# A state-space convolution and a mixer MLP on one core: weights by signed length and angle, constants on Pool, one ScalarE table ahead of the first turn

## The chip, the cores and the metric

The kernel runs on one core of one Trainium2 chip. The metric is device time in microseconds of one execution, lower is better; shown is the median of several runs. The kernel before takes 714.86 us (three runs, 712.22 to 715.42).

## The reference

Two blocks work on a sequence of 2048 positions with 512 channels, each scaled and shifted by values that come from a condition vector. The first block is a long convolution whose kernel K is the sum of 128 damped oscillations per channel. Cut to what matters:

```
mod = (silu(c) @ w_mod).reshape(1, 6, 1, 512)           # w_mod is 512 x 3072
sa, ca, ga, sb, cb, gb = mod[:, 0], ..., mod[:, 5]
h = layernorm(x) * (1 + ca) + sa
# first block: A, B, C are complex, 512 x 128
dt = exp(log_dt)
P  = exp((dt * A)[:, :, None] * l[None, None, :])       # l = 0 .. 2047
K  = einsum("dn,dnl,dn->dl", C, P, dt * B).real         # 512 x 2048
y  = irfft(rfft(h, padded) * rfft(K, padded)) + h * Dskip
x  = x + ga * y
h  = layernorm(x) * (1 + cb) + sb
x  = x + gb * mixer(h)      # spatial shift, then a channel MLP 512 -> 1376 -> 512
```

For the change it matters that the weight of one oscillation, w = C * B * dt, is complex. The kernel writes it as a length times a turn by an angle: the length multiplies the exponential's magnitude, the angle is added to the phase of the oscillation, and the oscillation is then one sine.

## The kernel before, in words

All the code is in `body`, in stages. The diff lies in the first.

Preparation (lines 285 to 409, a schedule written by hand: the order of the calls is the order on each engine). SP loads log_dt, c and the six raw arrays of A, B and C; Pool waits for one of them (`gate`) and then loads constant matrices (PA, CE, C0, PB, C1) on its own queue. VectorE builds two constants, MG and ON, in `cst`, then dt (`exp_exact`), then `la` (log magnitude per step) and `tf`, `t64` (phase per step and per 64 steps, each reduced by `frac` to a fraction of a turn), then the weight w as `wr`, `wi`. `hi` (a copy on ScalarE that rounds) and `lo` (a subtraction on VectorE) split each into two parts in `hilo`. `place` and `parts` are matmuls with 0/1 matrices that move these parts to the layout of later matmuls: TES (magnitudes), T0S (phase per step) and T1S (phase per 64 steps and the weight's angle). `exps` makes exponentials of magnitudes, four of 1024 columns and one of 768.

The angle of w is found from min/max of |wr| and |wi|: an arctangent of their quotient (`at0`), and then corrections by octant and quadrant with three masks `sg`, `sw`, `si`. The length is max * cos + min * sin of that arctangent, `wn`.

Modulation: `load_mod(n)` loads a 512-column block of w_mod (1 MB), `mod_parts(n)` multiplies it with the condition in four column groups and copies the result, `mod_sum(n)` adds the four groups. Blocks 0 to 2 are needed by the first block.

Rounds (`for k in range(33)`): `turns(k, cos)` makes the phase of one group of oscillations in PSUM, with rounding to whole turns by adding and subtracting the constant MAGIC = 1.5 * 2^23 through matmuls with ON and MG, and ScalarE takes the sine; `products(k)` on VectorE multiplies with the exponentials; `burst(k)` sums over oscillations by matmuls into K, held in the tile KX. Two `turns` run ahead of `products`. Each step of a turn is a pair of matmuls: l0 (phase per step, 32 rows of each group, zero-padded in the constant C0 to 64) into one half of a PSUM tile, l1 (64 rows of the other half of the array) into the other half. Between the rounds `side[k]` places the normalisation of u, its transforms, and more loads. After the rounds come the transforms of K and u, the products, the inverse transform and the mixer.

`psx` has two buffers: `turns`, `exps` and `parts` share them.

Of the kernel before, what the change touches and what calls it, by code (L numbers as in the profile page):

```python
# [14 lines left out]
MAGIC = 12582912.0  # L15
# [12 lines left out]
def shape_constants():  # L28
# [35 lines left out]
    c0 = np.tile((eye[:, :, None] * (j + .5)).reshape(16, 512), (2, 1))  # L64
    C0 = np.zeros((2, 2, 32, 2, 512))
    C0[:, 0, :, 0], C0[:, 1, :, 1] = c0, c0
    C0 = C0.reshape(128, 1024)
# [44 lines left out]
def body(ctx, tc, A):  # L112
# [6 lines left out]
    def act(out, in_, f=AF.Copy, scale=1.0, bias=0.0):  # L119
        return S.activation(out, in_, f, bias=bias, scale=scale)  # L120
# [73 lines left out]
    C0 = ph.tile([128, 1024], F32R, name="C0")  # L194
    C1 = ph.tile([128, 512], F32R, name="C1")
    CE = ph.tile([128, NXC], F32R, name="CE")
    C0N = ph.tile([128, 1024], F32R, name="C0N")
    C1N = ph.tile([128, 512], F32R, name="C1N")
    MG = ph.tile([128, 512], F32R, name="MG")
    ON = ph.tile([128, 3, 128], F32R, name="ON")  # L200
# [80 lines left out]
    def frac(x, r):  # L281
        V.tensor_scalar(r, x, MAGIC, MAGIC, op0=OP.add, op1=OP.subtract)
        V.tensor_sub(x, x, r)

    with tc.manual_schedule():
# [12 lines left out]
        V.memset(DS, 0.0)  # L298
# [4 lines left out]
        for r in (32, 96):  # L303
            V.memset(cst[r:r + 32], 1.0)
        V.tensor_copy(MG, cst)
        V.memset(cst[:, :384], 0.0)
        for i, (r, v) in enumerate(((0, 1.0), (0, -1.0), (32, 0.25))):
            for q in (r, r + 64):
                V.memset(cst[q:q + 1, i * 128:i * 128 + 128], v)
        V.tensor_copy(ON.rearrange("p a b -> p (a b)"), cst[:, :384])  # L310
        V.tensor_scalar(ld[:, 4:], cT, -1.0, None, op0=OP.mult)
        ex = exp_exact(pp, ld, [128, 8], "dt")
        dt = ex[:, :4]
# [24 lines left out]
        lo(0, tf)  # L338
# [3 lines left out]
        place(TES, 6, PA)  # L342
# [4 lines left out]
        V.tensor_mul(wr, cr, br)  # L347
        V.tensor_mul(t0, ci, bi)
        lo(2, t64)
        V.tensor_sub(wr, wr, t0)  # L350
        V.tensor_mul(wi, cr, bi)
        V.tensor_mul(t1, ci, br)
        V.tensor_add(wi, wi, t1)
        exps(0, 0, 5)
# [4 lines left out]
        def parts(i0, i1):  # L359
            for v in range(4):  # L360
                for i in range(i0, i1):
# [4 lines left out]
        ax, ay, mn = cr, br, tmp("mn")  # L366
        V.scalar_tensor_tensor(ax, wr, -1.0, wr, op0=OP.mult, op1=OP.max)
        V.scalar_tensor_tensor(ay, wi, -1.0, wi, op0=OP.mult, op1=OP.max)
        mx, mc = tmp("mx"), tmp("mc")
        V.tensor_tensor(mc, ax, ay, op=OP.max)  # L370
        V.tensor_scalar(mx, mc, 1e-37, None, op0=OP.max)
        V.reciprocal(mx, mx)
        V.tensor_tensor(mn, ax, ay, op=OP.min)
        V.tensor_mul(mx, mn, mx)
        at, at0 = tmp("at"), tmp("at0")
        act(at0, mx, AF.Arctan)
        act(at, at0, scale=INV2PI)
        act(wn, at0, AF.Sin, scale=-1.0, bias=hpi)
        act(ws, at0, AF.Sin)
        mp = [mod_parts(n) for n in range(2)]  # L380
        for f in mp:
            f()
        for n in range(2):
            mod_sum(n)()
        load_mod(2)
        load_u(0)
        sg, sw, si = la, t0, t1
        V.tensor_tensor(sg, ay, ax, op=OP.is_gt)
        V.tensor_scalar(sg, sg, -2.0, None, op0=OP.mult)
        V.tensor_scalar(sw, wr, 0.0, -2.0, op0=OP.is_lt, op1=OP.mult)  # L390
        V.tensor_scalar(si, wi, 0.0, -2.0, op0=OP.is_lt, op1=OP.mult)
        V.scalar_tensor_tensor(at, sg, 1.0, at, op0=OP.add, op1=OP.mult)
        V.scalar_tensor_tensor(at, sg, -0.125, at, op0=OP.mult, op1=OP.add)
        V.scalar_tensor_tensor(at, sw, 1.0, at, op0=OP.add, op1=OP.mult)
        V.scalar_tensor_tensor(at, sw, -0.25, at, op0=OP.mult, op1=OP.add)
        V.scalar_tensor_tensor(at, si, 1.0, at, op0=OP.add, op1=OP.mult)
        V.scalar_tensor_tensor(at, tf, 31.5, at, op0=OP.mult, op1=OP.add)
        frac(at, rr)
        hi(4, at)
        lo(4, at)  # L400
        parts(2, 4)
        for i in range(2):
            act(T1S.rearrange("p (t v) n -> p v t n", v=4)[:, 2 * i:2 * i + 2],
                px[i].rearrange("p (v t n) -> p v t n", v=2, t=4))
        V.tensor_mul(wn, wn, mc)
        V.tensor_mul(ws, ws, mn)
        V.tensor_add(wn, wn, ws)
        V.tensor_tensor(as4(wn), as4(wn), by(dt), op=OP.mult)
    pr.close()
# [38 lines left out]

    def turns(k, cos):
        t, u = divmod(k, 4)  # L450
        r0 = slice(u // 2 * 64, u // 2 * 64 + 64)
        r1 = slice(64 - r0.start, 128 - r0.start)
        l0, l1, c = T0S[r0, t], T1S[r1, t * 2 + k % 2], slice(k % 2 * 512, k % 2 * 512 + 512)
        x = psx.tile([128, 1024], F32, name="xx")
        ops = [(l0, C0[r0, c], l1, C1[r1])] + [(ON[r0, i], MG[r0], ON[r1, i], MG[r1]) for i in (2, 0, 1)[1 - cos:]]
        ops.append((l0, C0N[r0, c], l1, C1N[r1]))
        for i, (la, ma, lb, mb) in enumerate(ops):
            T.matmul(x[:, :512], la, ma, start=(i == 0), stop=(i == len(ops) - 1))  # L458
            T.matmul(x[:, 512:], lb, mb, start=(i == 0), stop=(i == len(ops) - 1))  # L459
# [80 lines left out]
    with tc.manual_schedule():  # L540
# [3 lines left out]
        for i in range(4):  # L544
            T.transpose(wps[:, i * 128:i * 128 + 128], wn[:, i * 128:i * 128 + 128], ident)
        act(WN, wps)
        late = mod_parts(2)
        turns(1, 0)
        late()
        late = mod_sum(2)  # L550
        turns(1, 1)
        late()
        load_u(1)
        for k in range(33):
            now, later = later, []
# [30 lines left out]
            for f in side[k]:  # L586
                f()
# [682 lines left out]
```

## Time and profile before

| | |
|---|---|
| median of 3 runs | 714.86 us (712.22 to 715.42) |
| profiled execution: its time | 714.44 us |
| its span, first to last instruction | 712.6 us |
| TensorE clock granted, mean | 0.994 |
| busy in the span | TensorE 669.5 us, VectorE 506.6, ScalarE 335.5, Pool 86.7 |
| 0 to 13 us | TensorE 0, VectorE 10.40, ScalarE 2.54 us busy |
| 13 to 38 us | TensorE 18.10, VectorE 22.44, ScalarE 17.64 us busy |

PE is TensorE's matmuls, PEld its weight loads, DVE is VectorE, ACT is ScalarE, SP issues DMAs. A row of the timeline begins with its start and its busy time in us, then engine, line, operation, out<-in and shapes; what stands in brackets is the idle time before it and what ended it. A matmul's end is modelled, so it is its start that counts. A mark like 64*128 behind a matmul is the rows and columns of the array that it uses. Line numbers are those of the kernel before; L120 is the helper for all of ScalarE's activations.

### The profile page before, as it was taken

The numbers are of one execution on the slowest core, as the hardware profiler recorded it, in microseconds if no ns is written. First come the engines' busy times: TensorE is split into PE (matmuls) and PEld (weight loads), VectorE is DVE, ScalarE is ACT, GpSimd is POOL, SyncE is SP. The second block draws the span as 40 slices with busy tenths as digits, with TensorE's granted clock in tenths as the row PEclk, the third lists the DMA queues.
The fourth block names the chain that finished last, engine by engine and source line by source line (L and its number), as shares of the span: only waits on it lengthen the run. The fifth ranks groups of instructions, "written<-read, shape, count | busy, mean of one in ns | idle before, by whom it ended". The sixth has DMA issues, their size and how long they took to land.

```text
span 712.6 us, 16838 instructions
## 1 busy us (share of the span) xinstructions
PE 669.5 (94%) x7083; PEld 516.9 (73%) x7083; DVE 506.6 (71%) x847; ACT 335.5 (47%) x549; POOL 86.7 (12%) x191
## 2 busy tenths in 40 slices
PE   2689999999999999998999899999999999999997
PEld 1256555656569665664688889999898988989896
DVE  8889999999996666866988868557464636454422
ACT  3769888889866444533344623314123221212120
POOL 1011211112000000000473100101010000000000
PEclk9899999999999999999999999999999999999999
DMA  8451374653439999874659201011020101111011
GB/s 280 145 144 52 91 218 101 181 139 94 141 75 332 237 301 302 267 241 152 204 176 319 90 22 39 16 45 31 27 63 16 53 22 31 31 30 30 0 30 30
DMA packets 56627, 85.51 MB, mean 120 GB/s; under 512 B 5508, under 2 KB 43400, under 8 KB 54888
## 3 DMA queue, kind: packets, MB, share of 16 engines
q1 hardware_dynamic: 52536, 66.87, 33.2%
q0 software_dynamic: 3136, 16.52, 6.5%
q8 instruction: 56, 0.92, 0.6%
q10 hardware_dynamic: 880, 1.05, 0.5%
q14 instruction: 19, 0.16, 0.1%
HBM read 58.20 MB, written 31.85 MB: 126 GB/s over the span
## 4 chain that ended last, share of the span: by engine, by line
PE 47%; DMA 2%; DVE 2%; ACT 1%; issue 1%; SPq 1%; ACTq 0%; DVEq 0%
PE pm L824 7%; PE pm L825 7%; PE pm L827 7%; PE pa L948 6%; PE pa L940 6%; PE pa L941 6%; PE ph L878 2%; PE ph L879 2%; PE ph L881 2%; PE pT L789 2%; DMA ld<-ZT 1%; DMA GD<-go 1%; PE pT L1138 1%; PE py L721 1%; DMA win<-GD 0%
## 5 line engine op out<-in xcount | busy, mean ns | idle before, releaser
L120 ACT ACTIVATE gh<-pm 128x512 fp32r<-128x512 f32 (+1 forms) x48 | 26.9, 561 | 200.6 <-PE pm L827 200.6
L824 PE MATMUL pm<-nh,w3h 128*128 128x256 f32 (+1 forms) x352 | 85.8, 279 | 0.9 <-ACT nh L120 0.9
L825 PE MATMUL pm<-nh,w3l 128*128 128x256 f32 (+1 forms) x352 | 85.6, 279 | 0.1
L932 DVE TENSOR_TENSOR gl<-gf,gh 128x512 fp32r<-128x512 f32 (+1 forms) x48 | 30.9, 643 | 68.3 <-ACT gf L120 68.3
L940 PE MATMUL pa<-w4h,gh 128*128 128x512 f32 (+1 forms) x176 | 69.6, 395 | 0.0
L941 PE MATMUL pa<-w4l,gh 128*128 128x512 f32 (+1 forms) x176 | 68.9, 392 | 0.0
L824 PEld LDWEIGHTS pm<-nh,w3h 128*128 128x128 f32 (+1 forms) x352 | 65.3, 185 | 2.6 <-ACT nh L120 1.1
L825 PEld LDWEIGHTS pm<-nh,w3l 128*128 128x128 f32 (+1 forms) x352 | 65.2, 185 | 2.2 <-DVE w3l L743 0.5
L827 PE MATMUL pm<-nl,w3h 128*128 128x256 f32 (+1 forms) x352 | 54.8, 277 | 0.0
L948 PE MATMUL pa<-w4h,gl 128*128 128x512 f32 (+1 forms) x176 | 48.1, 390 | 0.8 <-DVE gl L932 0.8
L458 PE MATMUL xx<-MG,ON 64*128 64x512 f32 x160 | 47.0, 389 | 0.0
L459 PE MATMUL xx<-MG,ON 64*128 64x512 f32 x160 | 47.0, 389 | 0.0
L827 PEld LDWEIGHTS pm<-nl,w3h 128*128 128x128 f32 (+1 forms) x352 | 46.6, 185 | 0.2 <-DVE nl L797 0.2
L752 POOL TENSOR_TENSOR rs<-mv,eps_t 128x1 f32<-128x1 f32 (+1 forms) x39 | 11.9, 306 | 278.0 <-DVE mv L758 266.1
L884 DVE TENSOR_TENSOR h<-h,ph 128x512 f32<-128x512 f32 x16 | 11.0, 688 | 45.1 <-PE ph L881 45.1
L476 DVE SCALAR_TENSOR_TENSOR e<-tr,p 128x512 f32<-128x512 f32 x64 | 41.1, 683 | 1.8 <-ACT tr L120 1.8
L120 ACT ACTIVATE z<-pz 128x512 f32<-128x512 f32 x32 | 17.4, 594 | 51.4 <-issue 21.7
L677 DVE TENSOR_TENSOR ma<-pk,us 128x512 f32<-128x512 f32 x32 | 21.9, 686 | 26.8 <-issue 15.8
L508 PEld LDWEIGHTS kp<-e,e 128*32 128x32 f32 x2048 | 30.1, 110 | 12.9 <-issue 7.2
L948 PEld LDWEIGHTS pa<-w4h,gl 128*128 128x128 f32 (+1 forms) x176 | 33.0, 188 | 8.3 <-DVE gl L932 1.2
L485 DVE TENSOR_TENSOR e<-tr,p 128x1024 f32<-128x1024 f32 x32 | 39.0, 1218 | 0.0
L486 DVE TENSOR_TENSOR e<-tr,m 128x1024 f32<-128x1024 f32 x32 | 39.0, 1218 | 0.0
(234 smaller groups left out, 1755.6 us busy)
## 6 DMA issues: line engine op xcount, KB each, us to landing
VU<-vs SPq DMA_DIRECT2D x64, 128.0 KB, 3.2
ld<-VU SPq DMA_DIRECT2D x16, 512.0 KB, 14.1
ZT<-z POOLq DMA_DIRECT2D x15, 512.0 KB, 7.1
ld<-ZT SPq DMA_DIRECT2D x12, 512.0 KB, 5.5
Dw<-in_w POOLq DMA_DIRECT2D x8, 688.0 KB, 4.7
xu<-in_u SPq DMA_DIRECT2D x16, 256.0 KB, 5.7
KX<-in_u SPq DMA_DIRECT2D x16, 256.0 KB, 12.3
GD<-go SPq DMA_DIRECT2D x16, 256.0 KB, 2.5
```

Of the source, the lines that this page charges most:

```text
L120: return S.activation(out, in_, f, bias=bias, scale=scale)
L458: T.matmul(x[:, :512], la, ma, start=(i == 0), stop=(i == len(ops) - 1))
L459: T.matmul(x[:, 512:], lb, mb, start=(i == 0), stop=(i == len(ops) - 1))
L476: V.scalar_tensor_tensor(e0[:, 1, a], tr[:, 1, 0], 1.0 - 2.0 * a, mg[:, a], op0=OP.mult, op1=OP.mult)
L485: V.tensor_mul(e0[:, 0], tr[:, 0, 0:1].to_broadcast([128, 2, 512]), mg)
L486: V.tensor_mul(e1.rearrange("p r d q -> p r (d q)"), tr[:, :, 1], m1s[0][:, u % 2:u % 2 + 1].to_broadcast([128, 2, 512]))
L824: T.matmul(p, wh[:, k, c], hi[k], start=(k == 0), stop=False)
L825: T.matmul(p, wl[:, k, c], hi[k], start=False, stop=False)
L827: T.matmul(p, wh[:, k, c], lo[k], start=False, stop=(k == 3))
L940: T.matmul(acc[i], gh[:m, e, s], W4h[:m, f], start=(f == 0), stop=False)
L941: T.matmul(acc[i], gh[:m, e, s], W4l[:m, f], start=False, stop=False)
L948: T.matmul(acc[i], gl[:m, e, s], W4h[:m, f], start=False, stop=(f == 10))
```

## The change

Five things are done at once.

- The angle is taken to the nearer axis: the larger of wr and wi becomes the signed divisor, so the quotient is signed and its arctangent lies within an eighth of a turn; a quarter turn is added where wi is larger (`sg`). The half turn for a negative divisor is left out, as the length keeps its sign. Two predicated copies take the place of the chain of corrections; |wr|, -wr and |wi| are made on ScalarE.
- MG and ON are built on Pool. MG is the same in all rows, and ON exists in two forms, for 32 rows and for 64.
- C0 has 512 columns in place of 1024. `turns` takes the 32 rows of l0 alone, beside the 64 rows of l1 in the other half.
- Modulation blocks 0 to 2 are loaded into KX, K's tile, behind the load of Dskip; both first tiles of u are loaded right behind them. `mod_sum` 0 and 1 and all of block 2 move behind the first turns.
- One element of sine ahead of the arctangent makes one table serve both.

```diff
-    C0 = np.zeros((2, 2, 32, 2, 512))
-    C0[:, 0, :, 0], C0[:, 1, :, 1] = c0, c0
+    c0 = np.tile((eye[:, :, None] * (j + .5)).reshape(16, 512), (4, 1))
+    C0 = np.tile(c0, (2, 1))
...
     def load_mod(n):
-        wmt[n] = (up if n < 3 else wml).tile([128, 4, 512], F32, name="xu" if n < 3 else "wm")
+        wmt[n] = KX[:, n * 2048:n * 2048 + 2048].rearrange("p (a b) -> p a b", a=4) if n < 3 else \
+            wml.tile([128, 4, 512], F32, name="wm")
...
-        load_mod(0)
-        load_mod(1)
-        V.memset(DS, 0.0)
-        for j in range(4):
-            Y.dma_start(DS[32 * j:32 * j + 1], A["dk"][j:j + 1])
+        P.memset(cst, MAGIC / 3)
+        P.tensor_copy(MG, cst)
+        for j in range(2):
+            P.memset(cst[:, :384], 0.0)
+            for i, v in enumerate((3.0, -3.0, 0.75 / MAGIC)):
+                for q in range(0, 128, 32 + 32 * j):
+                    P.memset(cst[q:q + 1, i * 128:i * 128 + 128], v)
+            P.tensor_copy(ON[:, j].rearrange("p b c -> p (b c)"), cst[:, :384])
-        V.memset(cst, MAGIC)
...
         frac(tf, rr)
+        V.memset(DS, 0.0)
+        for j in range(4):
+            Y.dma_start(DS[32 * j:32 * j + 1], A["dk"][j:j + 1])
+        load_mod(0)
+        load_mod(1)
+        load_mod(2)
+        load_u(0)
+        load_u(1)
...
-        place(T0S, 0, PA)
+        lo(0, tf)
+        act(ax, wr, AF.Abs)
+        act(nr, wr, scale=-1.0)
+        act(ay, wi, AF.Abs)
         exps(0, 0, 5)
+        place(T0S, 0, PA)
+        act(t31, tf, scale=31.5)
         act(C0N, C0.bitcast(F32), scale=-1.0)
         act(C1N, C1.bitcast(F32), scale=-1.0)
+        act(ws[:, :1], hpi, AF.Sin)
...
-        parts(0, 2)
...
+        parts(range(4), 0)
+        mp = [mod_parts(0)]
+        V.tensor_tensor(mc, ax, ay, op=OP.max)
+        V.tensor_tensor(sg, ay, ax, op=OP.is_gt)
+        V.copy_predicated(wr, sg, wi)
+        V.scalar_tensor_tensor(rc, mc, 1e-37, wr, op0=OP.is_lt, op1=OP.add)
+        V.reciprocal(rc, rc)
+        V.copy_predicated(wi, sg, nr)
+        V.tensor_mul(rc, rc, wi)
+        V.scalar_tensor_tensor(t31, sg, 0.25, t31, op0=OP.mult, op1=OP.add)
+        act(at0, rc, AF.Arctan)
+        lo(2, t64)
+        parts(range(4), 1)
+        mp.append(mod_parts(1))
+        mp[0]()
+        V.scalar_tensor_tensor(at, at0, INV2PI, t31, op0=OP.mult, op1=OP.add)
+        frac(at, t0)
+        hi(4, at)
+        mp[1]()
+        lo(4, at)
+        parts((0, 1), 2, 3)
+        parts((2, 3), 2, 3)
         act(wn, at0, AF.Sin, scale=-1.0, bias=hpi)
         act(ws, at0, AF.Sin)
+        T1v = T1S.rearrange("p (t v) n -> p v t n", v=4)
+        for i in range(2):
+            act(T1v[:, i], px[0].rearrange("p (v t n) -> p v t n", v=2, t=4)[:, i])
+        act(T1v[:, 2:], px[1].rearrange("p (v t n) -> p v t n", v=2, t=4))
...
     def turns(k, cos):
         t, u = divmod(k, 4)
-        r0 = slice(u // 2 * 64, u // 2 * 64 + 64)
-        r1 = slice(64 - r0.start, 128 - r0.start)
+        r0 = slice(u * 32, u * 32 + 32)
+        r1 = slice(64 - u // 2 * 64, 128 - u // 2 * 64)
...
-        ops = [(l0, C0[r0, c], l1, C1[r1])] + [(ON[r0, i], MG[r0], ON[r1, i], MG[r1]) for i in (2, 0, 1)[1 - cos:]]
+        ops = [(l0, C0[r0], l1, C1[r1])] + [(ON[r0, 0, i], MG[r0], ON[r1, 1, i], MG[r1]) for i in (2, 0, 1)[1 - cos:]]
...
-        late = mod_parts(2)
+        ms = [mod_sum(n) for n in range(2)]
         turns(1, 0)
-        late()
-        late = mod_sum(2)
+        for f in ms:
+            f()
         turns(1, 1)
-        late()
-        load_u(1)
+        later.append(mod_parts(2))
+        late = [lambda: later.append(mod_sum(2))]
```

Three places in the order of instructions. ScalarE, from the copies to TES to the first sine of a turn; `p` are the exponentials, `xu` and `KX` with `pu` copies of modulation parts, `KX` with `tp_at` the sines for the length, `modu` modulation sums. Before:

```order
L120 ACTIVATE p_250<-xx 128x768
L120 ACTIVATE C0N<-C_105 128x1024
L120 ACTIVATE C1N<-C_106 128x512
L120 ACT_TABLE_LOAD
L120 ACTIVATE tp_at_298<-tp_mx 128x512
L120 ACTIVATE tp_at<-tp_at_298 128x512
L120 ACT_TABLE_LOAD
L120 ACTIVATE KX<-tp_at_298,hpi 128x512
L120 ACTIVATE KX<-tp_at_298 128x512
L120 ACTIVATE xu<-pu 128x512 x2
L120 ACTIVATE modu<-pu 128x512 x2
L120 ACTIVATE hilo<-tp_at 128x512
```

The same stretch after:

```order
L118 ACTIVATE p_265<-xx 128x768
L118 ACTIVATE T0S<-pu 128x4x128 x2
L118 ACTIVATE tp_rr<-tp_tf 128x512
L118 ACTIVATE C0N<-C_105 128x512
L118 ACTIVATE C1N<-C_106 128x512
L118 ACT_TABLE_LOAD
L118 ACTIVATE KX<-hpi 128x1
L118 ACTIVATE tp_at_316<-tp_rc 128x512
L118 ACTIVATE KX<-pu 128x512
L118 ACTIVATE hilo<-tp_at 128x512
L118 ACTIVATE KX<-pu 128x512
L118 ACTIVATE KX<-tp_at_316,hpi 128x512
```

The angle's `hilo` stood behind a second table load, both sines and four modulation copies; now it stands behind one copy, and the sines come after it.

TensorE, from the exponentials to the first turn; `PB` are `parts`, `scb` is `mod_parts`, `sp_91` is `mod_sum`. Before:

```order
L257 MATMUL xx<-CE,TES 128x512 x8
L252 MATMUL xx<-CE,TES 128x512
L252 MATMUL xx<-CE,TES 128x256
L362 MATMUL xx<-hilo,PB 128x512 x8
L221 MATMUL pu<-xu,scb 32x512 x8
L228 MATMUL pu<-xu,sp_91 128x512 x2
L362 MATMUL xx<-hilo,PB 128x512 x8
L458 MATMUL xx<-C_105,T0S 128x512
```

After:

```order
L251 MATMUL xx<-CE,TES 128x256
L319 MATMUL pu<-hilo,PA 128x512 x4
L368 MATMUL xx<-hilo,PB 128x512 x4
L220 MATMUL pu<-KX,scb 32x512 x4
L368 MATMUL xx<-hilo,PB 128x512 x4
L220 MATMUL pu<-KX,scb 32x512 x4
L368 MATMUL xx<-hilo,PB 128x512 x8
L454 MATMUL xx<-C_105,T0S 128x512
```

The second quarter of `parts` now stands behind modulation block 0 and the second half behind block 1, and the sums have gone to behind the first turns.

SP's queue, where each DMA waits for those ahead of it. Before:

```order
L295 DMA FU<-in_FU 128x256
L214 DMA xu<-in_wm 128x4x512 x2
L300 DMA DS<-in_dk 1x128 x4
L301 DMA FK<-in_FK 128x128
L214 DMA xu<-in_wm 128x4x512
L238 DMA xu<-in_u 32x2048 x8
```

After:

```order
L294 DMA FU<-in_FU 128x256
L303 DMA FK<-in_FK 128x128
L328 DMA DS<-in_dk 1x128 x4
L213 DMA KX<-in_wm 128x4x512 x3
L237 DMA xu<-in_u 32x2048 x8
L440 DMA VU<-vs 64x2x256 x12
```

The modulation blocks stand behind the load of `DS`, which waits for VectorE to have cleared it.

More of the change, by code (lines that the diff above doesn't have):

```diff
@@ L193, in body @@
     TES = ph.tile([128, 8, 128], F32R, name="TES")
-    C0 = ph.tile([128, 1024], F32R, name="C0")
+    C0 = ph.tile([128, 512], F32R, name="C0")
     C1 = ph.tile([128, 512], F32R, name="C1")
     CE = ph.tile([128, NXC], F32R, name="CE")
-    C0N = ph.tile([128, 1024], F32R, name="C0N")
+    C0N = ph.tile([128, 512], F32R, name="C0N")
     C1N = ph.tile([128, 512], F32R, name="C1N")
     MG = ph.tile([128, 512], F32R, name="MG")
-    ON = ph.tile([128, 3, 128], F32R, name="ON")
+    ON = ph.tile([128, 2, 3, 128], F32R, name="ON")
     WN = ph.tile([128, 512], F32, name="WN")
@@ L337, in body @@
         hi(2, t64)
-        lo(0, tf)
+        place(TES, 6, PA)
         V.tensor_scalar(ex[:, 4:], ex[:, 4:], 1.0, None, op0=OP.add)
@@ L353, in body, with parts @@
         V.tensor_add(wi, wi, t1)
+        ax, ay, nr, t31 = cr, br, ci, rr
+        lo(0, tf)
+        act(ax, wr, AF.Abs)
+        act(nr, wr, scale=-1.0)
+        act(ay, wi, AF.Abs)
         exps(0, 0, 5)
+        place(T0S, 0, PA)
+        act(t31, tf, scale=31.5)
         act(C0N, C0.bitcast(F32), scale=-1.0)
         act(C1N, C1.bitcast(F32), scale=-1.0)
+        act(ws[:, :1], hpi, AF.Sin)
         px = [psx.tile([128, 1024], F32, name="xx") for i in range(2)]
-        def parts(i0, i1):
-            for v in range(4):
-                for i in range(i0, i1):
+        def parts(vs, *js):
+            for i in js:
+                for v in vs:
@@ L372, in body @@
[L372 to L377, printed above, removed]
+        parts(range(4), 0)
+        mp = [mod_parts(0)]
+        sg, mc, rc, at, at0 = la.bitcast(I32), tmp("mc"), tmp("rc"), tmp("at"), tmp("at0")
+        V.tensor_tensor(mc, ax, ay, op=OP.max)
+        V.tensor_tensor(sg, ay, ax, op=OP.is_gt)
+        V.copy_predicated(wr, sg, wi)
@@ L391, in body @@
[L391 to L397, printed above, removed]
@@ L407, in body @@
+        V.tensor_mul(wn, wn, wr)
+        V.tensor_mul(ws, ws, wi)
         V.tensor_add(wn, wn, ws)
@@ L450, in turns @@
         t, u = divmod(k, 4)
-        r0 = slice(u // 2 * 64, u // 2 * 64 + 64)
-        r1 = slice(64 - r0.start, 128 - r0.start)
-        l0, l1, c = T0S[r0, t], T1S[r1, t * 2 + k % 2], slice(k % 2 * 512, k % 2 * 512 + 512)
+        r0 = slice(u * 32, u * 32 + 32)
+        r1 = slice(64 - u // 2 * 64, 128 - u // 2 * 64)
+        l0, l1 = T0S[r0, t], T1S[r1, t * 2 + k % 2]
         x = psx.tile([128, 1024], F32, name="xx")
-        ops = [(l0, C0[r0, c], l1, C1[r1])] + [(ON[r0, i], MG[r0], ON[r1, i], MG[r1]) for i in (2, 0, 1)[1 - cos:]]
-        ops.append((l0, C0N[r0, c], l1, C1N[r1]))
+        ops = [(l0, C0[r0], l1, C1[r1])] + [(ON[r0, 0, i], MG[r0], ON[r1, 1, i], MG[r1]) for i in (2, 0, 1)[1 - cos:]]
+        ops.append((l0, C0N[r0], l1, C1N[r1]))
         for i, (la, ma, lb, mb) in enumerate(ops):
@@ L560, in body @@
                 turns(k + 2, 1)
+            while late:
+                late.pop()()
             if k < 32:
```

36 lines of the change are left out of this document (removed).

## The prediction

> **What bounds the kernel now.** I read the page first (slices), then sums over two windows, then the order of time through the first 41 us, then DMA landings.
>
> ```profile
> PE   2689999999999999998999899999999999999997
> DVE  8889999999996666866988868557464636454422
> ...
> 13.00:38.00 25.00, 18.10 (x54) 8.76 (x54) 22.44 (x37) 17.64 (x24) 0.00 (x0) 0.86 0.61 215
> ...
> 40.50:212.00 171.50, 163.93 (x2829) 102.06 (x2827) 168.68 (x219) 146.83 (x175) 26.66 (x40) 1.00 0.45 120
> ...
> L476 DVE SCALAR_TENSOR_TENSOR e<-tr,p x64: 658/684/693, 40.5 to 209.0; 128x512 f32<-128x512 f32 x64
> ```
>
> The diff touches the preparation, which ends with the first turn, and the inside of each turn. TensorE is nearly idle in the first two slices (17.8 us each) and full from the third on. From 40.5 to 212 us, the 32 rounds that make K, VectorE is busy 168.68 of 171.50 us and TensorE 163.93. The first product of these rounds is at 40.53 us, and VectorE never rests after it; what is behind it is TensorE at nine tenths or more. So whatever the preparation loses moves the whole rest, one to one, and a round has almost no room for a longer turn: (171.50 - 163.93) / 32 = 0.24 us on TensorE.
>
> The preparation, in order of time:
>
> ```profile
> 0.98 0.17 DVE L298 MEMSET DS<- 128x128 f32 x1
> 1.21 0.42 SPq L286 DMA_DIRECT2D ld<-in_ld  x1
> ...
> 6.05 0.16 DVE L311 TENSOR_SCALAR ld<-cT 128x4 f32<-128x4 f32 x1
> ...
> 9.16 0.68 DVE L329 TENSOR_TENSOR tp_la<-raw_ar,dt_o 128x512 f32<-128x512 f32 x1
> ...
> 13.09 3.95 PE L326 MATMUL pu<-hilo,PA 128*128 128x512 f32 x8 [13.09 <-DMA PA<-in_PA]
> ...
> 14.77 0.69 DVE L347 TENSOR_TENSOR tp_wr<-raw_cr,raw_br 128x512 f32<-128x512 f32 x1
> ...
> 15.17 0.60 ACT L120 ACTIVATE TES<-pu 128x512 fp32r<-128x512 f32 x1 [0.26 <-PE pu L326]
> 15.38 0.68 DVE L348 TENSOR_TENSOR tp_t<-raw_ci,raw_bi 128x512 f32<-128x512 f32 x1
> ...
> 17.89 3.78 ACT L120 ACTIVATE p<-xx 128x1024 f32<-128x1024 f32 x4 [0.21 <-PE xx L257]
> 18.50 0.69 DVE L353 TENSOR_TENSOR tp_wi<-tp_wi,tp_t 128x512 f32<-128x512 f32 x1
> ...
> 21.62 3.35 DVE L372 RECIPROCAL tp_mx<-tp_mx 128x512 f32<-128x512 f32 x1
> ...
> 22.56 1.05 ACT L120 ACTIVATE C0N<-C 128x1024 fp32r<-128x1024 f32 x1
> ...
> 24.15 1.28 ACT L120 ACT_TABLE_LOAD   x1
> ...
> 26.28 0.63 ACT L120 ACTIVATE tp_at<-tp_mx 128x512 f32<-128x512 f32 x1 [0.85 <-DVE tp_mx L374]
> ...
> 28.88 0.72 ACT L120 ACTIVATE KX<-tp_at,hpi 128x512 f32<-128x512 f32 x1
> ...
> 32.71 0.69 DVE L283 TENSOR_TENSOR tp_at<-tp_at,tp_rr 128x512 f32<-128x512 f32 x1
> ...
> 34.19 0.60 ACT L120 ACTIVATE modu<-pu 128x512 f32<-128x512 f32 x1 [1.11 <-PE pu L228]
> 34.69 0.62 ACT L120 ACTIVATE hilo<-tp_at 128x512 fp32r<-128x512 f32 x1
> ...
> 38.16 0.50 PE L458 MATMUL xx<-C,T0S 64*128 64x512 f32 x1 [0.18 <-ACT T1S L120]
> ...
> 39.40 1.03 ACT L120 ACTIVATE tr<-xx 128x1024 f32<-128x1024 f32 x1 [0.36 <-PE xx L459]
> ...
> 40.53 1.29 DVE L476 SCALAR_TENSOR_TENSOR e<-tr,p 128x512 f32<-128x512 f32 x2 [1.84 <-ACT tr L120]
> ...
> 44.88 1.12 PE L228 MATMUL pu<-xu,sp 128*128 128x512 f32 x2 [1.66 <-ACT xu L120]
> ```
>
> Three things bound it in turn: VectorE at the start (constants until 6.05), ScalarE's exponentials and tables from 17.89 to 26.28, then the angle's long correction on VectorE up to 32.71 + 0.69 = 33.40, and behind that ScalarE, which gets to the angle (34.69) only after the modulation sums.
>
> **The change part by part.**
>
> *Constants leave VectorE.* Its first work on data (6.05) then waits for cT alone. The ld transfer is issued at 1.21 and lands 1.7 us later (row below); cT is issued some 0.5 us behind it, so about 3.4. From L311 to the first product with A is 9.16 - 6.05 = 3.11 us, so that product starts at 6.5: minus 2.65. Then wr: one hi/lo subtraction moves behind wi (minus 0.61, the spacing of 14.77 and 15.38), the clearing of DS comes in (plus 0.17): 14.77 becomes 11.65, and wi, six operations less the other moved subtraction, ends at 15.4 instead of 19.19.
>
> ```profile
> L846 POOL COPY win<-go 128x384 f32<-128x384 f32 x2 | 1.0, 504 | 0.0
> ...
> L849 POOL MEMSET win<- 128x4 f32 x2 | 0.2, 106 | 0.0
> ...
> L150 POOL TENSOR_TENSOR lur<-lum,eps_t x16: 188/555/569, 47.1 to 185.9; 128x1 f32<-128x1 f32 x16
> ```
>
> On Pool the constants are three wide clearings and three casts (about 0.5 us each, as the copy) and 18 one-row fills (0.11): 5 us, behind Pool's own DMA issues. A one-column Pool operation takes 0.19 us alone and 0.56 in the busy rounds, so I allow three times: 15 us, done by about 24. They are needed at the first turn. Cost on the path: nothing, covered by 6 us. What Pool does to VectorE meanwhile no row shows for wide operations; L476 keeps 658 to 693 ns beside small Pool work, so I bound it by 0 and, if all 5 us of Pool held VectorE up by a third, 1.7 us, and take 0.4.
>
> *Loads move.* The two modulation blocks, 1 MB each, are now queued on SP behind the four rows of DS, hence behind VectorE's clearing of DS (about 9.2): issued at about 11, with the third block and u behind them. PA, CE and PB on the Pool queue have the engines more to themselves.
>
> ```profile
> 4.82 0.51 SPq L289 DMA_DIRECT2D raw_bi<-in_bi  x1
> ...
> xu<-in_wm SPq DMA_DIRECT2D x2, 1024.0 KB, 17.6
> ...
> raw_bi<-in_bi SPq DMA_DIRECT2D x1, 256.0 KB, 5.7
> PA<-in_PA POOLq DMA_DIRECT2D x1, 256.0 KB, 6.7
> ...
> ld<-in_ld SPq DMA_DIRECT2D x1, 2.0 KB, 1.7
> ```
>
> PA is what TensorE waits for at 13.09. Its bytes compete with those of the raw arrays, the last of which lands at 4.8 + 5.7 = 10.5; it comes not much before 11 and no later than now, and I take 11.7. The second copy to TES then ends at 14.4 (15.77 - 13.09 = 2.7 behind PA). ScalarE next makes |wr|, -wr and |wi|, about 0.55 us each, the last behind wi: free at 16.05. The exponentials start there, against 17.89.
>
> *ScalarE up to the arctangent.* Now: five exponentials 4.7 us (17.89 to 22.56), two copies to T0S, which came earlier before, the scaled tf, C0N at half size, C1N (five at 0.6), one table load 1.28, one element of sine about 0.25: 9.2 us, so the arctangent is at 25.2 instead of 26.28. VectorE has its quotient ready by then: maximum, comparison, a predicated copy, one more, the reciprocal 3.35, a copy, a product from 16.1 are about 7.3 us, 23.4. The predicated copy is not in the trace; the rows of this width lie between 0.62 on ScalarE and the reciprocal's 3.35. I take the two-input row, 0.69, which reads the same number of operands but one; at 3.35 each the two would be 5.3 us longer, of which the 1.8 us in hand cover a third and 3.5 would show.
>
> *From arctangent to angle.* Before: 34.69 - 26.28 = 8.4 us (a rescaling, a second table, two sines, two copies and two sums of modulation on ScalarE, twelve operations on VectorE). After: arctangent 0.63, one combination 0.69, rounding 1.1, semaphores: 2.5. This is the gain, 5.9 us. PB's second and third parts stand on TensorE behind modulation blocks 0 and 1: with 17.6 us to land as before they come at 28.7, a little late; with the constants' queue nearly empty by 20 I take 24.5, in time (the angle is at 27.7).
>
> *Angle to the first turn.* Before 38.16 - 34.69 = 3.47. After, hi 0.62, a modulation copy 0.55, both sines (0.72 and 0.61) stand ahead of the copies to T1S, which come in halves: 3.55. From the turn to the product 40.53 - 38.16 = 2.37, unchanged. The two modulation sums (TensorE 2 x 1.12, ScalarE 2 x 0.60, 3.4 us) now lie between turns 0 and 1; VectorE then has the first round's products to do (168.68 / 32 = 5.3 us a round), so they cost nothing; without that cover they would cost 3.4.
>
> Sum: arctangent -1.1, angle -5.9, copies +0.1, Pool +0.4: -6.5 us.
>
> *The turns.* Nine pairs a round, four for the sine and five for the cosine. Before, both of a pair use 64 rows; now the first uses 32 and the second the 64 of the other half.
>
> ```profile
> 61.50 0.39 PE L459 MATMUL xx<-MG,ON 64*128 64x512 f32 x1
> 61.51 0.39 PE L458 MATMUL xx<-MG,ON 64*128 64x512 f32 x1
> 61.72 0.39 PE L459 MATMUL xx<-MG,ON 64*128 64x512 f32 x1
> ...
> 57.74 0.50 PE L492 MATMUL kp<-CE,TES 128*128 128x512 f32 x1
> 58.17 0.73 PE L257 MATMUL xx<-CE,TES 32*128 32x512 f32 x2
> ```
>
> The two of a pair start 0.01 us apart, the later one of the program first, and a pair takes 0.22: the two row groups run as separate streams. If they stay separate the turns cost what they did. That 32 and 64 rows run beside each other no row shows: each change of tile size here is between tiles that share rows. A matmul between two such changes occupies 0.43 us (57.74 to 58.17), so the cost per pair lies between 0 and 2 x 0.43 - 0.22 = 0.64. I take 0, the row nearest to it in rows used: L458 and L459 have disjoint rows before and after.
> [...]
>
> **The rivals.**
> *Unequal tiles exclude each other.* Every pair then costs 0.2 (only in sequence) to 0.64 us (drained, weights not loaded ahead) more. Nine pairs a round: 1.9 to 5.8 us, less 0.24 of room, in 32 rounds: +53 to +178, less the 6.5: 761 to 886 us; with the lone matmul's price, 886. It decides against the change from 0.05 us a pair on (0.24 / 9 is free, 6.5 / 288 the gain). For it: the 0.43 us. Against it: the streams overtake each other, so what holds a matmul back is its own row group.
> *The modulation blocks land late.* Parts of T1S stand behind them on TensorE. Landing 17.6 us after issue, as before, costs 1.5 us (709.5); each us after that is one more, and from 30.5 us on nothing measurable is left: 712. For it: 1 MB beside a busy Pool queue took 17.6. Against: that queue has 0.25 MB less, and a start of 5 us.
> *The start of the rounds starves.* If the sums between turns 0 and 1 hold VectorE, 3.4 us of the gain go: 711. Against: 5.3 us of cover.
>
> **How the numbers follow.** The profiled execution took 714.44 us, 0.4 under the median of 714.86, with a span of 712.6. 714.4 - 6.5 = 708. No difference that can be measured is within 0.5%, 3.6 us. Chances: forecast 0.62, late blocks 0.12, starving 0.06, unequal tiles 0.20. The forecast's own bounds: PA as late as now +1.3, Pool 1.3 more than taken, or the predicated copies +3.5; on the other side an earlier PA, no Pool cost and shorter copies, -2.5: 705 to 711.5. With the second and third case the range goes to 715; the first rival is left out, it is 0.2. Faster: the forecast and half of the second and third case, 0.71; same: the other half, 0.09; slower 0.20.
>
> **What would show it.** Right: L304 at about 3.4 us, TensorE's first matmul before 12.5, one table load ahead of the arctangent at about 25, the first turn near 31 and the first product near 33.7, pairs still 0.22 us apart, the rounds still 171 us. Wrong: turns in which one matmul starts where the other ends; TensorE idle before PB's second or third part for a modulation block; VectorE resting in the first two rounds; VectorE's wide rows above 0.69 us while Pool fills.

## The result, and the profile after

The changed kernel takes 1088.33 us (median of four runs, 1080.21 to 1091.06) against 715.01 us: 1.5215 times as long, interval 1.5125 to 1.5305. The profiled execution took 1087.35 us, with a span of 1085.6 us and a mean granted clock of 0.766. Line numbers of the changed kernel are a few lower: its turns are L454 and L455 (before L458 and L459), its first product L472 (L476), its activations L118.

The page of the changed kernel, busy slices and three groups:

```profile
span 1085.6 us, 16851 instructions
...
PE   4999999999999999999999999999999999999998
...
DVE  8423323232413333232333667688865655544541
...
PEclk9655555555565565655657999999999999999999
...
L472 DVE SCALAR_TENSOR_TENSOR e<-tr,p 128x512 f32<-128x512 f32 x64 | 41.4, 688 | 334.5 <-PE kp L504 229.0
L455 PE MATMUL xx<-MG,ON 64*128 64x512 f32 x160 | 121.9, 762 | 0.0
L454 PE MATMUL xx<-MG,ON 32*128 32x512 f32 x160 | 121.1, 757 | 0.0
```

A slice is now 27.1 us long. Slices 2 to 21 are the rounds: VectorE, which hardly rested there before, is mostly at two or three tenths and waits 334.5 us ahead of its products, most of it for TensorE; TensorE is full; and the granted clock, which stood at 1.00 before, is at five or six tenths. The products themselves cost what they did (688 ns, before 683). It is TensorE's matmuls of the turns that are long: 757 and 762 ns each.

The same in sums over the stretches, the rounds of the changed kernel in the first row and everything behind them in the second (length, then TensorE, weight loads, VectorE, ScalarE, Pool busy, granted clock, DMA share, GB/s):

```profile
37.00:580.40 543.40, 542.98 (x2767) 238.21 (x2766) 169.96 (x217) 150.24 (x175) 16.00 (x40) 0.53 0.13 35
580.40:1085.00 504.60, 490.85 (x4260) 409.68 (x4256) 306.63 (x550) 167.47 (x347) 56.72 (x141) 1.00 0.37 111
```

Before, from the first product at 40.53 us to the last, the rounds took 169.2 us, and 502.9 us lay behind them. So the loss, 374 us, is in the rounds, with some 2 us of difference behind them. Ahead of them the change gained:

```profile
3.33 0.17 DVE L304 TENSOR_SCALAR ld<-cT 128x4 f32<-128x4 f32 x1 [1.95 <-DMA cT<-in_c]
...
10.11 0.71 DVE L281 TENSOR_SCALAR tp_rr<-tp_t 128x512 f32<-128x512 f32 x1
...
11.65 2.04 PE L319 MATMUL pu<-hilo,PA 128*128 128x512 f32 x4 [11.65 <-DMA PA<-in_PA]
...
12.01 0.69 DVE L346 TENSOR_TENSOR tp_wr<-raw_cr,raw_br 128x512 f32<-128x512 f32 x1
...
14.55 0.99 DVE L350 TENSOR_TENSOR tp_t<-raw_ci,raw_br 128x512 f32<-128x512 f32 x1
...
16.84 1.92 ACT L118 ACTIVATE p<-xx 128x1024 f32<-128x1024 f32 x2
...
26.55 0.61 ACT L118 ACTIVATE tp_at<-tp_rc 128x512 f32<-128x512 f32 x1
...
29.11 0.63 ACT L118 ACTIVATE hilo<-tp_at 128x512 fp32r<-128x512 f32 x1 [1.46 <-DVE tp_at L282]
...
32.42 0.49 PE L454 MATMUL xx<-C,T0S 32*128 32x512 f32 x1 [0.24 <-ACT T1S L118]
32.84 0.49 PE L455 MATMUL xx<-C,T1S 64*128 64x512 f32 x1
33.26 0.50 PE L454 MATMUL xx<-MG,ON 32*128 32x512 f32 x1
...
35.38 0.50 PE L455 MATMUL xx<-C1N,T1S 64*128 64x512 f32 x1
...
37.02 1.29 DVE L472 SCALAR_TENSOR_TENSOR e<-tr,p 128x512 f32<-128x512 f32 x2 [3.41 <-ACT tr L118]
38.40 0.79 PE L455 MATMUL xx<-MG,ON 64*128 64x512 f32 x1
39.12 0.79 PE L454 MATMUL xx<-MG,ON 32*128 32x512 f32 x1
```

The first turn starts at 32.42 us, 5.7 us earlier than before. But already in it the second matmul of a pair starts about where the first ends, 0.42 us later and not 0.01. At 38.40 us the step has become 0.72 us: the clock has gone down as well, from 1.00 (32.4 to 35.9 us) to 0.50 (38.3 to 41.0 us).

So two things have to be told apart: what makes the two of a pair wait for each other, and what takes the clock.

### The profile page after: what moved, and what is told of

The parts are those of the page before. It is cut to its first block, busy times and chain, and to the rows that moved or that the text cites. A ratio compares the mean times of both kernels' runs of the same rounds, so it can differ in the third digit from the quotient of the medians.

```text
span 1085.6 us, 16851 instructions
## 1 busy us (share of the span) xinstructions
PE 1053.4 (97%) x7083; PEld 657.8 (61%) x7083; DVE 503.9 (46%) x827; ACT 339.0 (31%) x553; POOL 83.8 (8%) x215
## 5 line engine op out<-in xcount | busy, mean ns | idle before, releaser
L472 DVE SCALAR_TENSOR_TENSOR e<-tr,p 128x512 f32<-128x512 f32 x64 | 41.4, 688 | 334.5 <-PE kp L504 229.0
L455 PE MATMUL xx<-MG,ON 64*128 64x512 f32 x160 | 121.9, 762 | 0.0
L454 PE MATMUL xx<-MG,ON 32*128 32x512 f32 x160 | 121.1, 757 | 0.0
L118 ACT ACTIVATE tr<-xx,hpi 128x1024 f32<-128x1024 f32 x32 | 35.6, 1114 | 194.1 <-PE xx L455 194.1
L118 ACT ACTIVATE gh<-pm 128x512 fp32r<-128x512 f32 (+1 forms) x48 | 26.9, 561 | 200.6 <-PE pm L825 200.6
L455 PEld LDWEIGHTS xx<-MG,ON 64*128 64x128 f32 x160 | 43.7, 273 | 66.7 <-issue 66.7
L454 PEld LDWEIGHTS xx<-MG,ON 32*128 32x128 f32 x160 | 43.3, 270 | 66.7 <-issue 66.7
L118 ACT ACTIVATE tr<-xx 128x1024 f32<-128x1024 f32 x32 | 32.8, 1024 | 136.1 <-issue 66.4
L504 PE MATMUL kp<-e,e 128*32 128x64 f32 x2048 | 61.0, 311 | 0.0
L455 PE MATMUL xx<-C1N,T1S 64*128 64x512 f32 x64 | 49.3, 770 | 0.0
L454 PE MATMUL xx<-C,T0S 32*128 32x512 f32 x64 | 47.9, 748 | 0.2 <-ACT T1S L118 0.2
L454 PE MATMUL xx<-C0N,T0S 32*128 32x512 f32 x64 | 48.1, 751 | 0.0
```

Source lines behind the costliest of these rows:

```text
L472: V.scalar_tensor_tensor(e0[:, 1, a], tr[:, 1, 0], 1.0 - 2.0 * a, mg[:, a], op0=OP.mult, op1=OP.mult)
L504: T.matmul(kp[32 * j:32 * j + 32, (k % 2) * 4 + g], e1[:, r, d], e0[:, r, :, d * 32:d * 32 + 32], start=(r == 0), stop=(r == 1), skip_grou ...
```

## The experiments

The theories. **A**: tiles of 32 and of 64 rows can't be at work at once, and each change of size makes TensorE stand still for a while (drains it, as the expectations say); the clock falls because a drained TensorE does little. **B**: tiles of 32 rows are the trouble by themselves, mixed or not. **C**: the cause lies elsewhere in the change, in Pool's work or the loads. Beside each timed experiment the kernel before took 714 to 715 us (medians).

**Only the turns back to 64 rows.** The changed kernel with the pairs of before (32 rows zero-padded to 64):

```
-        r0 = slice(u * 32, u * 32 + 32)
+        r0 = slice(u // 2 * 64, u // 2 * 64 + 64)
         r1 = slice(64 - u // 2 * 64, 128 - u // 2 * 64)
...
+    C0[:, 0, :, 0], C0[:, 1, :, 1] = c0, c0      # zero-padded, 1024 columns; C0N alike, ON in one form
```

> The changed kernel with the turns of before: both matmuls of a pair on 64 rows, C0 zero-padded to 1024 columns, ON in its one 64-row form (Pool has 6 one-row fills instead of 18); all else as changed. Theory A (each change of tile size drains TensorE, and the drained TensorE then loses half of its clock): 708 to 710 us, the first turn near 32.5 us as in the changed kernel, pairs 0.22 us apart, granted clock 0.99 again. Theory B (32-row tiles are themselves slow or idle enough to lower the clock, whatever stands beside them): the same time. Theory C (the new preparation or the loads into K's tile cost it): about 1088 us still.

Measured: 711.02 us (707.18 to 713.71, twelve runs) against 714.22: ratio 0.9947, interval 0.9924 to 0.9971. Its turns and its rounds:

```profile
26.85 0.61 ACT L120 ACTIVATE tp_at<-tp_rc 128x512 f32<-128x512 f32 x1
...
32.73 0.50 PE L455 MATMUL xx<-C,T0S 64*128 64x512 f32 x1 [0.25 <-ACT T1S L120]
32.73 0.50 PE L456 MATMUL xx<-C,T1S 64*128 64x512 f32 x1
33.06 0.39 PE L455 MATMUL xx<-MG,ON 64*128 64x512 f32 x1
...
35.07 1.29 DVE L473 SCALAR_TENSOR_TENSOR e<-tr,p 128x512 f32<-128x512 f32 x2 [1.16 <-ACT tr L120]
...
35.10:205.00 169.90, 164.55 (x2819) 102.38 (x2823) 166.53 (x217) 147.52 (x177) 26.36 (x40) 0.99 0.42 113
```

The pairs run side by side again, the rounds take 169.9 us, the clock is 0.99. The rest of the change is a small gain, half a per cent: this kernel beats both. C falls.

**Only the turns of 32 rows, in the kernel before.**

```
+        r0 = slice(u * 32, u * 32 + 32)
...
+        ops = [(l0, C0[r0], l1, C1[r1])] + [(ON[r0, 0, i], MG[r0], ON[r1, 1, i], MG[r1]) ...]
```

> The kernel before with only the turns of the change: 32 rows beside 64, C0 of 512 columns, ON in two forms; these constants are built on VectorE where they stood, 18 one-row fills instead of 6, some 2.5 us more there. Theories A and B: 715 + 379 + 2.5, about 1095 us, clock 0.55 in the rounds. Theory C: about 717 us.

Measured: 1091.05 us, ratio 1.5275 (1.5204 to 1.5346). Its rounds:

```profile
45.90:586.60 540.70, 538.29 (x2764) 236.59 (x2763) 169.95 (x217) 148.85 (x173) 16.01 (x40) 0.54 0.14 37
```

The turns alone cause the loss, clock included.

**Fewer changes of size.** The changed kernel with the matmuls of a turn in other orders: all of 32 rows, then all of 64 (one change inside a turn); and 32, 64, 64, 32 (half the changes).

```
-        for i, (la, ma, lb, mb) in enumerate(ops):        # 32, 64, 32, 64, ...
+        for z in range(2):                                # grouped: 32, 32, ..., 64, 64, ...
+            for i, o in enumerate(ops):
...
+            for z in ((0, 1), (1, 0))[i % 2]:             # the other kernel: 32, 64, 64, 32, ...
```

> The changed kernel, but each turn issues all its 32-row matmuls and then all its 64-row ones: 2 changes of size in a turn instead of 8 or 10, and no two of a pair side by side. Theory A: 18 matmuls of 0.22 us in a round and 4 changes of 0.1, 4.3 us against 2.06, so some 2 us a round over what the other work hides: about 775 us, and the clock stays near 1. Theory B: half of the matmuls still use 32 rows, so the clock stays at 0.55 and the time above 1000 us.

> The changed kernel with the two sizes in the order 32, 64, 64, 32, 32, 64 and so on: half as many changes of size. Theory A: two matmuls between changes take 0.65 us at full clock instead of 0.85, 5.9 us a round against 7.7: about 820 us if the clock stays up, about 960 if it falls as in the changed kernel. Theory B: the clock as in the changed kernel, and near 1050 us.

Measured: 940.31 us (ratio 1.3164, 1.31 to 1.3229) and 1016.7 us (1.4234, 1.4149 to 1.4319). The rounds of the grouped kernel, and two rows of one of its turns (x3: three matmuls from that start on):

```profile
37.90:435.30 397.40, 396.17 (x2768) 229.84 (x2766) 169.81 (x217) 150.27 (x175) 16.73 (x40) 0.57 0.18 48
...
102.72 1.48 PE L455 MATMUL xx<-MG,ON 32*128 32x512 f32 x3
104.00 0.62 PE L455 MATMUL xx<-C0N,T0S 32*128 32x512 f32 x1
```

Those of the other order:

```profile
36.50:504.00 467.50, 466.41 (x2766) 218.09 (x2765) 169.96 (x217) 150.23 (x175) 16.49 (x40) 0.54 0.16 41
```

543, 467, 397 us of rounds as the changes become fewer: each change costs, as A has it. But for the grouped turns A said full clock and about 775 us, and the clock is 0.57, though matmuls of one size follow each other without a gap (three in 1.28 us, 102.72 to 104.00, 0.43 each, where a matmul took 0.22 at a clock of 1.00). The 0.57 is a mean: the turn ahead of this one, at 100.00 to 102.24 us, still runs at 0.23 us a matmul, this one at 0.43. So a drain is not what takes the clock, or not alone.

**Turns of 64 rows, grouped by halves.** The same order with equal tiles, to see whether the grouping by itself matters.

```
         # turns of 64 rows as in the first experiment
+        for z in range(2):
+            for i, o in enumerate(ops):
```

> The changed kernel with turns of 64 beside 64 rows (as e1_turns64), but each turn issues all matmuls of one half and then all of the other: no change of tile size, and the partners 4 or 5 instructions apart. Streams theory (each row group takes its instructions independently, so the second half overtakes): pairs side by side, 711 us. Queue theory (TensorE takes matmuls in program order and only neighbours overlap): 18 matmuls of 0.22 us one after the other, 2 us a round more, 775 us at full clock; and if half of the array working is what lowers the clock, as in e3_grouped, 900 us or more.

Measured: 723.49 us, ratio 1.0123 (1.0066 to 1.018). A sine turn's and a cosine turn's first matmuls, and the rounds:

```profile
102.39 0.49 PE L456 MATMUL xx<-C,T0S 64*128 64x512 f32 x1 [0.34 <-ACT p L120]
102.40 0.49 PE L456 MATMUL xx<-C,T1S 64*128 64x512 f32 x1
...
103.42 0.39 PE L456 MATMUL xx<-C,T0S 64*128 64x512 f32 x1
103.65 0.49 PE L456 MATMUL xx<-C,T1S 64*128 64x512 f32 x1
...
36.40:221.30 184.90, 179.70 (x2799) 116.76 (x2801) 167.28 (x217) 148.34 (x176) 26.30 (x40) 0.96 0.39 104
```

The two halves are separate streams indeed, as the prediction had it: a matmul four places later in the program starts 0.01 us behind its partner, one five places later one matmul (0.23 us) behind. Grouped by halves, turns of equal tiles take 1% longer than the kernel before, turns of unequal ones 32%.

**Full rows, and few rows.** Two kernels to part the clock from the drain: every matmul of a turn on 128 rows, one after the other, no change of size; and 32 beside 32 rows in pairs.

```
+        r0 = r1 = slice(0, 128)                              # full rows
...
+        r1 = slice((u ^ 2) * 32, (u ^ 2) * 32 + 32)          # the other kernel: 32 beside 32
```

> The changed kernel with both matmuls of each pair on all 128 rows, one after the other, and no change of size inside a turn; the sums take in rows of other groups (the selection of a group is left out), ON has one row. Drain theory of the clock (the clock falls because drained TensorE stands still between matmuls): it stays near 1, 18 matmuls of 0.22 us, 3.9 us a round against 2.06, less 0.24 of room: about 760 us. Rows theory of the clock (what counts is the share of the array's rows that work, averaged over some us): also near 1 and 760. Unequal-order theory (two matmuls that do not overlap are enough to lower it): 0.55 to 0.8 and 900 us or more.

> The changed kernel with 32 beside 32 rows: the second matmul of a pair takes only the first 32 of its 64 rows (half of l1's parts are left out), in another row group. No change of size, pairs can overlap, 64 of 128 rows work. Drain theory of the clock: pairs 0.22 us apart, clock near 1, 710 us. Rows theory: the pairs overlap but the clock falls as in e3_grouped, pairs 0.43 us apart at times, 800 to 850 us.

Measured: 775.18 us (ratio 1.0846, 1.0795 to 1.0898) and 768.2 us (1.0749, 1.0695 to 1.0803). Full rows, two matmuls of a turn and the rounds:

```profile
101.52 0.39 PE L451 MATMUL xx<-MG,ON 128*128 128x512 f32 x1
101.74 0.39 PE L452 MATMUL xx<-MG,ON 128*128 128x512 f32 x1
...
36.80:270.30 233.50, 228.24 (x2799) 156.60 (x2801) 168.94 (x217) 149.35 (x176) 22.30 (x40) 0.99 0.31 82
```

32 beside 32:

```profile
60.40 0.62 PE L454 MATMUL xx<-MG,ON 32*128 32x512 f32 x1
60.40 0.62 PE L455 MATMUL xx<-MG,ON 32*128 32x512 f32 x1
60.82 0.62 PE L454 MATMUL xx<-MG,ON 32*128 32x512 f32 x1
...
34.80:265.10 230.30, 224.12 (x2811) 137.48 (x2815) 168.42 (x217) 149.21 (x177) 20.28 (x40) 0.69 0.31 83
```

Two tiles of 32 rows do run side by side, so B's half about the pairing is wrong: it is the mix that excludes. But their clock is 0.69, and at 60.40 us a pair takes 0.42 us where 64 beside 64 took 0.22, with no change of size inside a turn. TensorE that works serially on all 128 rows keeps 0.99. So the clock is lower with few rows at work, 0.69 against 0.99, and not only where sizes change. The 0.69 is again a mean, of stretches like these two of 32 beside 32:

```profile
50.00:90.00 40.00, 39.04 (x428) 24.82 (x427) 27.64 (x37) 21.70 (x25) 4.70 (x8) 0.50 0.24 63
210.00:240.00 30.00, 29.04 (x477) 18.24 (x473) 27.08 (x36) 25.67 (x31) 3.88 (x8) 1.00 0.43 124
```

The turns are the same in both, once at a clock of 0.50 and once at 1.00. What brings the clock back was not tested.

**Full rows, drained.** If rows alone mattered, full rows with drains would keep the clock; if it is rows times the share of time they stream, they would not. Between neighbours of the kernel with full rows stands a matmul of two columns on 64 rows, fourteen a round:

```
         # full rows as above, and between two of them
+        T.matmul(x[:, 512:514], ON[64:, 0], MG[64:, :2], start=False, stop=False)
```

> e8_rows128 (all matmuls of a turn on 128 rows; the selection of a group is left out) with a matmul of 2 columns on 64 rows, of zero weights, between neighbours: 14 a round, two changes of size each. By the 0.43 us that a change each way takes, 6 us a round and the rounds 190 us longer than e8's 233: 425 us at full clock. Duty theory (the clock follows rows times working time, so standing still for a drain lowers it too): about half of the time lost, like 64 rows at work, so a clock as in e9_rows32_pairs, 0.6 to 0.75 in the rounds, and over 1050 us. Rows-only theory (the rows of the running matmuls count, not the pauses): clock above 0.95 and about 965 us.

Measured: 1134.12 us, ratio 1.5851 (1.5706 to 1.5996). Three neighbours, with the large matmuls' rows at 0.50 us as at a clock of 1.00 in the changed kernel (0.79 at 0.50), and the rounds:

```profile
102.26 0.50 PE L451 MATMUL xx<-MG,ON 128*128 128x512 f32 x1
102.69 0.27 PE L453 MATMUL xx<-MG,ON 64*128 64x2 f32 x1
102.89 0.50 PE L454 MATMUL xx<-MG,ON 128*128 128x512 f32 x1
...
39.50:620.60 581.10, 579.76 (x3209) 325.57 (x3208) 169.96 (x217) 150.45 (x175) 16.06 (x40) 0.63 0.13 33
```

A matmul and its small neighbour take 0.63 us where the matmul alone took 0.22: two changes of size cost 0.41 us, the small matmul's own time included, so some 0.2 each at most. And the clock goes to 0.63 although every large matmul uses all rows.

**The parts of the preparation.** Three variants of the kernel that beats both: the constants MG and ON back on VectorE; the one-element sine that asks for the table early left out; and modulation blocks 0 and 1 loaded right behind FU, ahead of the four rows of DS.

```
-            P.memset(cst[:, :384], 0.0)
+            V.memset(cst[:, :384], 0.0)             # the whole block for MG and ON likewise
...
-        act(ws[:, :1], hpi, AF.Sin)                 # the second kernel
...
+        load_mod(0)                                 # the third: behind FU's load
+        load_mod(1)
...
-        load_mod(0)                                 # and no longer behind the rows of DS
-        load_mod(1)
```

> e1_turns64 with its constants MG and ON built on VectorE again instead of Pool, at the place where the kernel before built them (6 one-row fills). If the move to Pool gains what the prediction counted, VectorE's first work on data goes from 3.3 to about 6 us, its wide rows near 10 us go back to 0.43 us, and the first turn comes 2 us later, 34.7 instead of 32.7: 713 us against 711. If VectorE's start is covered by PA and the raw loads: no difference.

> e1_turns64 without the one element of sine ahead of the arctangent: the table load before it then takes a set without sine, and a second load of 1.28 us stands before the two sines of the length, behind the angle. If ScalarE is what the first turn waits for there: the first turn 1.3 us later less the element's 0.2, 33.8 instead of 32.7. If TensorE's last parts cover it: no later than 32.9.

> e1_turns64 with modulation blocks 0 and 1 queued right behind FU as in the kernel before, still into K's tile. If they crowd PA as the prediction says, TensorE's first matmul goes from 12.05 to about 13.1 and the first turn a little over 1 us later, 33.8. If PA is bound by its own queue: no change of either. Total time within the spread in both cases.

Measured: constants on VectorE 711.06 us, ratio 0.9953 (0.9933 to 0.9973). Its first work on data and a wide row of `frac`:

```profile
4.53 0.16 DVE L305 TENSOR_SCALAR ld<-cT 128x4 f32<-128x4 f32 x1
...
11.17 0.43 DVE L283 TENSOR_SCALAR tp_rr<-tp_t 128x512 f32<-128x512 f32 x1
```

Its first turn is at 34.2 us, 1.5 us later; only part of that is the constants: the arctangent is 0.53 us later (27.38 against 26.85), and TensorE's last parts of T1S take 3.65 us against 2.38; why they do was not shown. At the end of the kernel no difference shows (711.06 against 711.02), though the intervals would hide 1.5 us. The row at 11.17 takes 0.43 us; beside Pool's clearings the same row took 0.71 (L281 above).

Without the early sine (one execution, 711.75 us) a second table load stands ahead of the sines:

```profile
30.48 1.28 ACT L120 ACT_TABLE_LOAD   x1
...
34.04 0.50 PE L454 MATMUL xx<-C,T0S 64*128 64x512 f32 x1 [0.34 <-ACT T1S L120]
```

The first turn comes 1.3 us later than 32.73, by the load's own 1.28. Up to the first turn, the table asked for in advance is worth one load.

With the modulation blocks early (one execution, 709.8 us):

```profile
7.74 0.98 SPq L215 DMA_DIRECT2D KX<-in_wm  x2
...
11.86 2.04 PE L322 MATMUL pu<-hilo,PA 128*128 128x512 f32 x4 [11.86 <-DMA PA<-in_PA]
```

PA lands as early as in the other two. So, by this one execution, the blocks' place behind the rows of DS is not what brings PA forward. They are still issued 1.1 us later than in the kernel before (7.74 against 6.61), so what does bring it forward stays open.

## Why the prediction was wrong

**The step that failed** is the one for the turns: "I take 0, the row nearest to it in rows used: L458 and L459 have disjoint rows before and after." Rows of 64 beside 64 were carried over to 32 beside 64. The runs showed in its place: tiles of 32 and of 64 rows take turns, though their rows are disjoint. A matmul between two others of another size takes 0.42 us at a clock of 1.00 (32.42 to 35.38 us, seven steps of the changed kernel), 18 of them in a round 7.6 us, where nine pairs took 2.0. The 0.43 us of the lone matmul, quoted and laid aside, was the price. From one matmul to the next it is 0.42 us where tiles of one size took 0.22, so 0.2 us a change, for disjoint rows too, and about as much in the kernel with full rows, drained (0.41 us for two changes). The weight loads (PEld) show it too: in the changed kernel each starts with its own matmul (both at 32.84 us, both at 33.26), 0.24 us after the load before it ended; in the kernel before, with equal tiles, the load starts 0.23 us ahead (60.12 us, for the matmul at 60.35).

**The rival was mis-sized.** Unequal tiles exclude each other, at the lone matmul's price, gave 886 us. That price, 0.64 us a pair, was an estimate; the changed kernel shows 0.62 at a clock of 1.00 (2 x 0.42 - 0.22). Of the rounds' 543 us that price explains about 340: 169 + 32 x (7.6 - 2.0 - 0.24). The remaining 200 us come with the granted clock, 0.53 in these rounds: at 0.50 a step takes 0.72 us and not 0.42, which in 18 x 32 steps makes about 170 of them. No term and no rival had it: the row for the rounds before shows a clock of 1.00, and the price was worked out as if it stayed there.

What takes the clock, from nine kernels. Rows at work is worked out: the rows of a matmul of a turn, both of a pair where they overlap, times the share of the time that it streams, taking 0.22 us of streaming at a clock of 1.00, a pair's spacing in the kernel before (in alternation 48 rows on average x 0.22 / 0.42; with half the changes 48 x 0.22 / 0.32, the mean of 0.42 and 0.22; drained 128 x 0.22 / 0.63; grouped 48 x 0.22 / 0.28, four matmuls in 1.12 us at 100.00 and at 101.12 us). All are estimates.

| turns of | rows at work | mean clock in the rounds | rounds, us |
|---|---|---|---|
| 32 and 64 in alternation (changed kernel) | 25 | 0.53 | 543 |
| the same in the kernel before | 25 | 0.54 | 541 |
| 32, 64, 64, 32 | 33 | 0.54 | 467 |
| 32s, then 64s | 38 | 0.57 | 397 |
| 128, drained | 45 | 0.63 | 581 |
| 32 beside 32 | 64 | 0.69 | 230 |
| 64 beside 64, grouped by halves | under 128 | 0.96 | 185 |
| 128, serial | 128 | 0.99 | 234 |
| 64 beside 64 | 128 | 0.99 | 170 |

Two things went with a lower clock, each without the other: fewer rows with no change of size in a turn (0.69), and changes of size with all rows in the large matmuls (0.63). So neither A's cause (drains alone) nor B's (32 rows alone) covers both. The mean clock rises with the rows at work through the table, which would fit rows at work as the one cause. But that is not shown. Over one stretch of every kernel, 40 to 200 us, the order breaks: 0.65 with 45 rows (128, drained) against 0.59 with 64 (32 beside 32). And 32 beside 32 runs at both clocks with the same turns. What holds is that the kernels near 128 rows keep the clock for nearly all of the rounds (means of 0.96 to 0.99) and those at 64 and fewer lose it for most (0.53 to 0.69). Whether rows, columns or data count was not tested, the rounds also hold matmuls that are no turns, and no threshold was measured. By the profile's busy share TensorE was busier in the slow rounds (542.98 of 543.40 us, at 0.53) than before (161.63 of 169.20 us, at 1.00), so that share does not tell the clock.

**The preparation**, point by point, from the changed kernel and the one with turns of 64 rows:

- First work on data at 3.33 us (forecast 3.4), wr at 12.01 (11.65), PA at 11.65 and 12.05 (11.7), exponentials at 16.84 (16.05), arctangent at 26.55 and 26.85 (25.2). Of the 1.35 us missing at the arctangent in the changed kernel, 0.8 is missing when the exponentials start. Pool has most of it: beside its clearings and casts VectorE's wide rows with one input took up to 0.71 us instead of 0.43, and two with two inputs 0.99 instead of 0.69. From the first product with A to the exponentials the kernel of 64 rows takes 10.38 us (6.35 to 16.73), the same with the constants on VectorE 9.71 (7.55 to 17.26), in one execution each: 0.7 us for Pool, where 0.4 was taken. The changed kernel, with more of Pool's fills, takes 10.51. The rest is ScalarE's own leg, 9.7 us from the exponentials to the arctangent where 9.2 were added up.
- From arctangent to angle 2.56 us (2.5), from the angle to the first turn 3.31 (3.55), from the turn to the product 2.34 in the kernel of 64 rows (2.37). These steps were right, and with them the largest gain, 5.9 us.
- The modulation sums between turns 0 and 1 cost next to nothing, as said: the rounds of the kernel with turns of 64 rows take 169.9 us against 169.2. Neither late blocks nor starving rounds came. The reason given for an earlier PA is not shown: with the blocks early it lands at 11.86.
- With turns of 64 rows the first product comes 5.46 us earlier (forecast 6.8: 40.53 less 33.7), and the total is 3.8 us less by the ratio, interval 2.1 to 5.4. That the whole would follow one to one is thus neither shown nor excluded: the stretch behind the rounds takes 500 to 506 us in single executions (511 in the drained kernel), and what of the gain goes there stays open.

## What to carry to other kernels

Before rows are taken out of matmuls, look at who runs beside them: here tiles of equal size on disjoint rows overlapped, tiles of 32 and 64 rows took turns and paid some 0.2 us a change, so zero rows that keep a pair equal can be the cheaper ones. And read the granted clock stage by stage and ask what keeps it up: matmuls on fewer rows, or changes of size, made TensorE no less busy in the profile, but the mean clock of all that it did in that stage was 0.53 to 0.69. A rival that would turn the sign deserves one small run, or at least its full price with the clock in it.

## What the runs showed of the hardware that was not expected

- Over the rounds, 32-row and then 64-row matmuls, back to back but for two changes a turn, had a mean clock of 0.57, pairs of 32 rows 0.69, 128 rows in series 0.99. Pairs of 32 rows ran at 0.50 from 50 to 90 us and at 1.00 from 210 to 240 us. In the changed kernel the clock fell some 5 us after the first turn (0.42 us a step up to 35.38, 0.72 from 38.40 on; clock 1.00 from 36 to 37 us, 0.65 from 37 to 38, 0.50 from 38 to 39) and was 1.00 again in the sum behind the rounds.
- In the turns of equal tiles grouped by halves, the stream of one half of the array overtook the other by four matmuls of the program (start 0.01 us apart), and not in full by five (0.23 us).
- Beside Pool's clearings and casts of 128 x 384 to 128 x 512 VectorE's wide rows with one input took up to 0.28 us more (0.43 to 0.71), two thirds; the prediction's bound was a third.
